# A fused attention and MLP kernel: another order table for its 1258 steps

## The chip, the cores and the metric

The kernel runs on one core of a Trainium2 chip. The metric is the time of one execution on the device in microseconds (us), the median of three runs. TensorE is called PE, VectorE DVE, ScalarE ACT, GpSimd POOL and SyncE SP, as in the profile.

## What is computed

The input `x` has 2048 tokens of 512 values. The result is `x + s * g`, where `s` is an attention over eight earlier tokens, two apart, and `g` a gated MLP, both of the same normalized input:

```python
xn = _layernorm(x)
qkv = (xn @ wqkv)                      # 32 heads of 16
logits = einsum("bhsd,bhswd->bhsw", q, kg) * scale   # kg: keys s, s-2, ..., s-14
o = einsum("bhsw,bhswd->bhsd", softmax(logits), vg)
s = o @ wo
y = _layernorm(xn)
g = silu(gelu(y @ w1 + b1) @ w2 + b2)  # 512 -> 1376 -> 512
return x + s * g
```

## The kernel before

Tokens are split by parity into two halves (c = 0, 1) of eight blocks of 128 tokens. Every multiplication of float32 values is made of three float16 ones: each operand is split into a high and a low part, scaled by a power of two that the kernel derives from a sum of squares (`total`, `half_exp`, `up`, `down`, L504 to L533).

The work comes in these pieces. `center` and `direct` (L673 to L691) make the first projections of two blocks directly in float32 from x, to give PE work while the other weights load. `y0` and `ln1` normalize the blocks and transpose them. `qkv` (L848 on PE) makes queries, keys and values of a unit, which is one half of the tokens and a group of eight heads; there are eight units. Its results leave PSUM by ACT (L866) or DVE (L862) into `U`. `attention` runs on DVE: products (L914), their sums (L917), softmax (L937 to L946, with the exponential on ACT, L940), products with the values (L972), sums of these shared by DVE (L967) and POOL (L982, L992), and a split for the output projection (L955 on ACT, L957 on DVE), whose result a DMA transposes (L960). `mlp1` (L1125 on PE, L1138 and L1141 on ACT, L1143 on DVE) and `mlp2` (L1161) are the MLP, for four chunks of 512 tokens and eleven slices of the hidden layer. `last_block` (L806 to L819; L806 and L807 pad on POOL) handles the narrow eleventh slice. `wo_first` and `wo_last` (L1038 and L1070 on PE) are the output projection.

`wo_last` ends the kernel. For each of the last eight blocks PE adds the last head group's share (L1070), DVE multiplies by the gate (L1102), DVE (L1109) or, for blocks 0, 2 and 4, POOL (L1106) adds x, and SP issues the store of the block (L1111). Block 7 is done in two halves of 256 columns, with a store each; the second one, the last half block, is multiplied in twelve matmuls of its own after everything else. So there are nine stores.

All DMAs are issued by SP. A DMA that waits for its data holds those behind it on SP. PSUM is used through rings of buffers: `ps` (three, for `qkv`, `mlp1` and some small totals), `pl` (one) and `z` (four). The products of attention use a ring of three buffers in SBUF (`prod`). 24 multiplications without use (L1279) fill PE's early waits.

The order of all this is not that of the code. `tile_mixer` only adds steps to a `Plan`, numbered in order of adding, each with its engine and what it reads and writes. `Plan.issue` then takes the steps in the order of the table `ORDER` and emits them; each engine executes its own steps in that order, and waits where data or a buffer isn't ready. When a step needs a new buffer of a ring, it gets the one that came free first by the table, so the table also decides which buffer serves what:

```python
order, fixed = [], [self.ops[n] for n in reversed(ORDER)]
...
            if fixed:
                o = fixed.pop()
```

Of the kernel before, what the change touches and what calls it, by code (L numbers as in the profile page):

```python
# [72 lines left out]
    0, 1, 2, 3, 4, 5, 6, 7, 8, 9, 10, 11, 19, 109, 117, 125, 114, 121, 130, 128, 108, 20, 123, 126, 129, 21, 33,  # L73
    32, 112, 22, 119, 23, 34, 24, 35, 25, 26, 54, 37, 38, 12, 13, 14, 15, 16, 17, 106, 107, 40, 49, 36, 68, 27,
    166, 47, 45, 41, 43, 28, 50, 51, 168, 115, 29, 30, 136, 31, 42, 53, 66, 56, 67, 69, 55, 57, 89, 167, 58, 62,
    70, 52, 71, 46, 72, 44, 90, 63, 169, 59, 137, 76, 64, 48, 18, 80, 170, 85, 65, 132, 73, 152, 74, 84, 86, 75,
    91, 87, 88, 60, 144, 178, 177, 138, 171, 139, 77, 173, 61, 153, 124, 154, 148, 149, 150, 120, 93, 78, 92,
    97, 98, 151, 175, 94, 81, 133, 99, 134, 174, 172, 181, 198, 95, 155, 82, 79, 145, 146, 116, 227, 228, 211,
    212, 213, 229, 214, 176, 182, 140, 141, 142, 179, 230, 135, 147, 100, 302, 96, 83, 306, 219, 203, 220, 221,
    143, 303, 304, 237, 180, 194, 196, 183, 156, 157, 158, 204, 205, 207, 208, 195, 197, 186, 190, 184, 159,  # L80
    305, 222, 187, 185, 39, 206, 191, 105, 160, 161, 192, 307, 308, 104, 101, 309, 102, 310, 314, 103, 238, 188,
    209, 210, 193, 385, 386, 199, 407, 200, 201, 408, 202, 242, 409, 111, 410, 113, 215, 216, 127, 400, 122,
    401, 217, 402, 110, 411, 412, 241, 218, 189, 239, 240, 387, 380, 413, 378, 403, 118, 414, 404, 415, 131,
    223, 243, 224, 225, 416, 417, 244, 405, 406, 256, 226, 246, 248, 382, 247, 249, 425, 441, 421, 422, 429,
# [12 lines left out]
    340, 344, 576, 526, 583, 567, 525, 341, 527, 647, 587, 646, 584, 597, 613, 342, 575, 348, 573, 615, 488,
    489, 598, 643, 586, 645, 644, 593, 654, 640, 1057, 641, 345, 594, 648, 349, 350, 614, 642, 346, 611, 612,
    652, 589, 595, 653, 660, 490, 596, 649, 590, 601, 602, 491, 351, 616, 618, 650, 617, 620, 619, 622, 347,
    499, 497, 353, 496, 352, 358, 514, 655, 651, 659, 591, 354, 355, 592, 656, 657, 623, 663, 661, 662, 671,  # L100
    668, 667, 670, 621, 626, 627, 628, 658, 492, 356, 624, 629, 630, 676, 599, 669, 678, 631, 632, 359, 664,
    672, 360, 665, 600, 679, 675, 677, 680, 673, 634, 633, 635, 361, 625, 357, 493, 606, 363, 362, 605, 579,
    368, 607, 681, 666, 637, 674, 682, 636, 683, 603, 685, 741, 737, 684, 686, 742, 694, 638, 604, 738, 364,
    695, 739, 692, 693, 365, 709, 710, 711, 366, 367, 609, 373, 577, 610, 608, 740, 712, 713, 688, 744, 757,
    748, 689, 758, 369, 746, 754, 743, 747, 749, 745, 702, 755, 753, 762, 773, 759, 714, 716, 715, 760, 718,
    719, 724, 717, 374, 375, 750, 370, 751, 725, 726, 371, 720, 721, 703, 727, 260, 722, 376, 372, 377, 723,
    728, 752, 729, 730, 690, 763, 756, 823, 764, 696, 691, 824, 698, 769, 697, 825, 699, 767, 771, 732, 731,
    733, 735, 826, 734, 736, 761, 829, 765, 700, 830, 837, 827, 828, 835, 831, 836, 701, 784, 832, 833, 704,
# [12 lines left out]
    1086, 1088, 1087, 1089, 1094, 1095, 1096, 961, 1019, 1097, 1090, 1032, 1030, 983, 924, 1020, 919, 925, 1098,
# [1351 lines left out]
```

## Time and profile before

| what | value |
|---|---|
| median of three runs (lowest to highest) | 420.45 us (419.94 to 420.98) |
| the profiled execution | 420.24 us |
| its span in the profile | 418.5 us |
| PE busy | 404.2 us, 97% |
| DVE busy | 386.4 us, 92% |
| ACT busy | 223.7 us, 53% |
| POOL busy | 129.3 us, 31% |
| DMA queue q1 | 51408 packets, 47.16 MB, 40.7% of 16 engines' span |

The span is the time from the first to the last recorded instruction of the core; the profiled execution's own time is 1.8 us longer. In a row of the timeline stand the start in us, the duration in us, the engine, the line of the kernel, the operation, what it writes and reads, and the count where like instructions were merged; in brackets at the end, how long the engine was idle before it and which instruction ended that. A row of the waits has who waited, for whom, the total in us, how many times, and the longest. A row of stretches has, after its length, the busy time of PE, PE's weight loads, DVE, ACT and POOL, then the granted clock of PE, the DMA share and GB/s. Starts of PE's multiplications overlap the ends of those before them by 0.16 us or so, since the array is a pipeline.

### The profile page before, as it was taken

What the parts mean: (1) busy time and instruction counts of PE and PEld (TensorE: products, weight loads), DVE (VectorE), ACT (ScalarE), POOL (GpSimd) and SP (SyncE); (2) the same over time, 40 slices, a digit from 0 to 9 for tenths busy, and PEclk for the clock granted to TensorE, in tenths of its full rate; (3) what the DMA queues carried; (4) which work ended last, traced back from release to release, by engine and by line L of the source; (5) the groups of instructions that cost most, each with busy time, mean ns of one, the idle gap of its engine ahead of it and who ended that gap; (6) DMA issues with size and microseconds to landing.
All of it is one profiled execution on the core that took longest, in us unless ns stands there. A gap on an engine that the chain in (4) does not pass through costs nothing.

```text
span 418.5 us, 5475 instructions
## 1 busy us (share of the span) xinstructions
PE 404.2 (97%) x2035; PEld 200.9 (48%) x2035; DVE 386.4 (92%) x379; ACT 223.7 (53%) x370; POOL 129.3 (31%) x140
## 2 busy tenths in 40 slices
PE   7999999999999999999999999999999999999991
PEld 4655544444444554554555554444455454444441
DVE  3998999999999999999989999999999989989972
ACT  3799998863768567435573361215432853162310
POOL 3820300061555352403333224232535250520021
PEclk9999999999999999999999999999999999999996
DMA  8938527340021372923148054310082439106334
GB/s 288 387 86 231 208 83 188 84 179 2 2 27 44 101 162 42 188 87 82 19 94 249 4 114 120 107 50 25 2 263 52 100 91 232 42 3 176 75 77 175
DMA packets 51435, 47.51 MB, mean 114 GB/s; under 512 B 36008, under 2 KB 36448, under 8 KB 50896
## 3 DMA queue, kind: packets, MB, share of 16 engines
q1 hardware_dynamic: 51408, 47.16, 40.7%
q8 instruction: 16, 0.26, 0.2%
q14 instruction: 11, 0.09, 0.1%
HBM read 24.11 MB, written 7.34 MB: 75 GB/s over the span
## 4 chain that ended last, share of the span: by engine, by line
PE 77%; DVE 15%; issue 4%; ACT 1%; DMA 1%; POOL 0%; DVEq 0%; ACTq 0%
PE ps L848 25%; PE z L1161 22%; PE ps L1125 18%; PE ps L1038 5%; PE ps L1070 2%; PE z L1070 2%; DVE L L917 2%; DVE w L560 2%; DVE prod L914 2%; DVE prod L972 2%; DVE h L1143 1%; PE pl L691 1%; DVE zsc L1349 1%; PE pl L848 1%; DVE wq L617 1%
## 5 line engine op out<-in xcount | busy, mean ns | idle before, releaser
L848 PE MATMUL ps<-wq,yT 128*128 128x384 f16 (+1 forms) x708 | 130.2, 337 | 0.9 <-DVE s L515 0.7
L1161 PE MATMUL z<-w,h 128*128 128x512 f16 x480 | 113.5, 379 | 0.0
L1125 PE MATMUL ps<-yT,w 128*128 128x512 f16 x480 | 110.4, 379 | 1.0 <-DVE ssq L515 1.0
L848 PEld LDWEIGHTS <-yT 128*128 128x128 f16 x744 | 72.5, 98 | 60.3 <-issue 1.8
L914 DVE TENSOR_TENSOR prod<-U 128x2048 f32<-128x2048 f32 x32 | 75.2, 2348 | 1.4
L1125 PEld LDWEIGHTS <-w 128*128 128x128 f16 x480 | 46.8, 98 | 56.2 <-issue 1.2
L917 DVE TENSOR_REDUCE L<-prod 128x128 f32<-128x2048 f32 x32 | 73.0, 2283 | 0.6
L1161 PEld LDWEIGHTS <-h 128*128 128x128 f16 x480 | 46.7, 98 | 54.3
L972 DVE TENSOR_TENSOR prod<-pl,U 128x2048 f32<-128x2048 f32 x28 | 63.4, 2283 | 3.1 <-POOL prod L982 2.8
L982 POOL TENSOR_TENSOR prod<-prod,prod 128x2048 f32<-128x2048 f32 x7 | 34.2, 4881 | 72.5 <-DVE prod L972 61.5
L1138 ACT ACTIVATE ps<-ps,b1T,hsc 128x512 f32<-128x512 f32 x40 | 29.7, 747 | 49.1 <-PE ps L1125 48.9
L866 ACT ACTIVATE U<-ps,cs 128x384 f32<-128x384 f32 x54 | 30.9, 576 | 38.4 <-PE ps L848 38.4
L991 POOL COPY gate<-prod 1x1 f32<-1x1 f32 x21 | 5.0, 240 | 112.2 <-DVE prod L914 102.0
L1141 ACT ACTIVATE h<-ps,hsc 128x512 f16<-128x512 f32 x40 | 27.1, 685 | 13.4 <-PE z L1161 12.1
L992 POOL TENSOR_TENSOR prod<-prod 128x1024 f32<-128x1024 f32 x14 | 32.9, 2348 | 0.0
L1143 DVE SCALAR_TENSOR_TENSOR h<-ps,hsc,h 128x512 f16<-128x512 f32 x40 | 29.4, 743 | 3.5 <-ACT h L1141 3.5
L1038 PE MATMUL ps<-wo,oT 128*128 128x512 f16 x96 | 21.9, 379 | 0.0
L967 DVE TENSOR_TENSOR prod<-prod,prod 128x2048 f32<-128x2048 f32 x9 | 20.6, 2290 | 0.2
L1138 ACT ACT_TABLE_LOAD x11 | 14.1, 1283 | 9.9 <-PE ps L1125 9.8
L955 ACT ACTIVATE o<-prod,osc 128x1024 f16<-128x1024 f32 (+1 forms) x9 | 9.4, 1049 | 15.6 <-DVE prod L967 10.3
L992 POOL TENSOR_TENSOR prod<-prod,prod 128x1024 f32<-128x1024 f32 x7 | 16.4, 2347 | 0.0
L1070 PEld LDWEIGHTS <-oT 128*128 128x128 f16 x108 | 10.6, 98 | 10.4
(188 smaller groups left out, 400.8 us busy)
## 6 DMA issues: line engine op xcount, KB each, us to landing
f<-in_A_x_dram SPq DMA_DIRECT2D x31, 256.0 KB, 3.2
U<-U SPq DMA_DIRECT2D x16, 392.0 KB, 3.9
gd<-f SPq DMA_DIRECT2D x12, 256.0 KB, 3.3
prod<-in_A_x_dram SPq DMA_DIRECT2D x8, 256.0 KB, 6.2
oT<-in_B_w_dram SPq DMA_DIRECT2D x2, 1024.0 KB, 9.8
yT<-in_B_w_dram SPq DMA_DIRECT2D x2, 1024.0 KB, 5.5
f<-gd SPq DMA_DIRECT2D x8, 256.0 KB, 3.4
out_dram<-f SPq DMA_DIRECT2D x8, 256.0 KB, 3.1
```

Source lines behind the costliest of these rows:

```text
L848: nc.tensor.matmul(b.t[:, 0:wide], y[:, s, k, o:o + P], wq[hb][:, t, k], start=(n == 0), stop=(n == 11))
L866: act(384, lambda i=i, b=b: nc.scalar.activation(U3[:, i:i + 31:15, :], b.t[:, 0:384].rearrange("p (t e) -> p t e", t=3), AF.Identity, sca ...
L914: dve(2048, lambda p2=p2, g=g: nc.vector.tensor_tensor(p2(), q, slots(Ut, KH, 2 * g), op=ALU.mult), qk + [("kh", ub, 0), ("kh", ub, 1), (" ...
L917: dve(2048, lambda pr=pr, g=g: nc.vector.tensor_reduce(L3()[:, 2 * g:2 * g + 2], pr.t.rearrange("p (r f d) -> p r f d", r=2, d=DH), AX.X, ...
L972: dve(2048, lambda: nc.vector.tensor_tensor(pr.t.rearrange("p (r f d) -> p r f d", r=2, d=DH), A3()[:, 2 * g:2 * g + 2].rearrange("p r (f ...
L982: pool(4.75, lambda: nc.gpsimd.tensor_tensor(acc.t, acc.t, p1.t, op=ALU.add), [acc, p1], [acc])
L992: nc.gpsimd.tensor_tensor(x.t[:, 0:1024], x.t[:, 0:1024], y(), op=ALU.add)
L1038: nc.tensor.matmul(b.t, oT[:, hb, i // 4, s, i % 4], wo[:, t, hb], start=(hb == 0 and n == 0), stop=(hb == last and n == 2))
L1125: nc.tensor.matmul(b.t[0:M], w1[:, s, f * 512 + k * M:f * 512 + (k + 1) * M], yT[ch][:, t, k], start=(n == 0), stop=(n == 11))
L1138: act(512, lambda: nc.scalar.activation(b.t[0:M], b.t[0:M], AF.Gelu_apprx_tanh, bias=b1T[0:M, f:f + 1], scale=hsc[0:M, 1:2]), [b, ("b1T",) ...
L1143: dve(512, lambda: nc.vector.scalar_tensor_tensor(lo()[0:M], b.t[0:M], hsc[0:M, 2:3], hi()[0:M], op0=ALU.mult, op1=ALU.subtract), [b, hk], ...
L1161: nc.tensor.matmul(z.t, hl[s][0:K, t * P:(t + 1) * P], w2[0:K, w, f], start=(f == 0 and n == 0), stop=(f == NF - 1 and n == 2))
```

## The change

The table `ORDER` is replaced by another order of the same 1258 numbers. Nothing else changes: the steps, their engines and what they compute are the same. The first and last lines of the table:

```diff
 ORDER = (
-    0, 1, 2, 3, 4, 5, 6, 7, 8, 9, 10, 11, 19, 109, 117, 125, 114, 121, 130, 128, 108, 20, 123, 126, 129, 21, 33,
+    0, 1, 2, 3, 4, 5, 6, 7, 8, 9, 10, 11, 19, 32, 33, 126, 128, 123, 115, 109, 20, 112, 114, 129, 21, 34, 22,
...
-    1237, 1256, 1252, 1228, 1257, 1248, 1223, 1253, 1243, 1233, 1238, 1218,
+    1233, 1218, 1248, 1243, 1223, 1253, 1254, 1255, 1256, 1237, 1238, 1257,
 )
```

What this moves on the engines is shown at three places.

SP, the nine stores that end the program (256 columns wide is a half of block 7, 512 a whole block). In brackets is what an instruction waits for, by engine; DMAHW is the queue's own place. Before:

```order
L1111 DMA out_dram<-U_88 128x512 [waits DMAHW2_49,Pool_49]
L1111 DMA out_dram<-U_88 128x256 [waits DMAHW3_49,DVE_49,Activation_49]
L1111 DMA out_dram<-U_88 128x512 [waits DMAHW4_49]
L1111 DMA out_dram<-U_88 128x512 [waits DMAHW5_49]
L1111 DMA out_dram<-U_88 128x256 [waits DMAHW6_49,DVE_49]
L1111 DMA out_dram<-U_88 128x512 [waits DMAHW7_49]
L1111 DMA out_dram<-U_88 128x512 [waits DMAHW0_49]
L1111 DMA out_dram<-U_88 128x512 [waits DMAHW1_49,Pool_49]
L1111 DMA out_dram<-U_88 128x512 [waits DMAHW2_49]
```

And now:

```order
L1111 DMA out_dram<-U_88 128x512 [waits DMAHW2_49,Pool_49]
L1111 DMA out_dram<-U_88 128x512 [waits DMAHW3_49,DVE_49]
L1111 DMA out_dram<-U_88 128x512 [waits DMAHW4_49,Pool_49]
L1111 DMA out_dram<-U_88 128x512 [waits DMAHW5_49,DVE_49]
L1111 DMA out_dram<-U_88 128x512 [waits DMAHW6_49,DVE_49]
L1111 DMA out_dram<-U_88 128x512 [waits DMAHW7_49]
L1111 DMA out_dram<-U_88 128x256 [waits DMAHW0_49,DVE_49]
L1111 DMA out_dram<-U_88 128x512 [waits DMAHW1_49,Pool_49]
L1111 DMA out_dram<-U_88 128x256 [waits DMAHW2_49,DVE_49]
```

The store of the last half block (step 1257) was second and is now last; that of block 4 (1238, added by POOL) was eighth and stands before it. By block the order was 2, last half, 6, 1, first half of 7, 5, 3, 4, 0, and is 2, 3, 0, 6, 5, 1, first half of 7, 4, last half. On PE, the three half-wide multiplications of the first half of block 7 (step 1250) stood between the last ones of block 4 (1235) and the final twelve (1254), and now stand before block 4's.

DVE, where the first attention unit meets the first `mlp1` steps (about 42 to 54 us before). L914 and L917 are products and sums of the attention, L1143 is the end of an `mlp1` step and frees its PSUM buffer. Before:

```order
L914 TENSOR_TENSOR prod_95<-U_88 128x2048
L917 TENSOR_REDUCE L_105<-prod_95 128x2x64
L931 MEMSET L_105 1x8
L914 TENSOR_TENSOR prod_96<-U_88 128x2048
L1143 SCALAR_TENSOR_TENSOR h_109<-ps_143,hsc,h_109 128x512
L914 TENSOR_TENSOR prod_97<-U_88 128x2048
```

And now:

```order
L914 TENSOR_TENSOR prod_96<-U_88 128x2048
L917 TENSOR_REDUCE L_105<-prod_96 128x2x64
L914 TENSOR_TENSOR prod_95<-U_88 128x2048
L917 TENSOR_REDUCE L_105<-prod_95 128x2x64
L1143 SCALAR_TENSOR_TENSOR h_109<-ps_142,hsc,h_109 128x512
L931 MEMSET L_105 1x8
```

A second L917 now stands ahead of the first L1143, which moved behind it. On PE the buffer ps_142 that this L1143 reads is taken next by an L848 group of two sets of four (steps 215 and 216), and four sets of three L1125 (400 to 403) and three sets of four L848 (223 to 225), which stood behind this group, now stand ahead of it.

DVE somewhat later (about 72 to 92 us before). L515 on `ssq` reads a total from a `ps` buffer and so frees it for PE. Before:

```order
L942 TENSOR_REDUCE mx_112<-L_105 128x64
L617 SCALAR_TENSOR_TENSOR wq_79<-yT_86,qsc,wq_79 128x2x384
L943 RECIPROCAL mx_112<-mx_112 128x64
L946 TENSOR_TENSOR pl_144<-L_105,mx_112 128x512
L972 TENSOR_TENSOR prod_97<-pl_144,U_88 128x2048
L617 SCALAR_TENSOR_TENSOR wq_79<-yT_86,qsc,wq_79 128x2x384
L1143 SCALAR_TENSOR_TENSOR h_110<-ps_141,hsc,h_110 128x512
L972 TENSOR_TENSOR prod_96<-pl_144,U_88 128x2048
L1143 SCALAR_TENSOR_TENSOR h_109<-ps_142,hsc,h_109 128x512
L1349 TENSOR_TENSOR zsc<-zsc,hsc 128x1
L917 TENSOR_REDUCE L_106<-prod_95 128x2x64
L515 TENSOR_SCALAR ssq<-ps_143 128x1
```

And now:

```order
L946 TENSOR_TENSOR pl_144<-L_105,mx_112 128x512
L1143 SCALAR_TENSOR_TENSOR h_108<-ps_142,hsc,h_108 128x512
L917 TENSOR_REDUCE L_106<-prod_95 128x2x64
L515 TENSOR_SCALAR ssq<-ps_142 128x1
L522 TENSOR_SCALAR s_124<-ssq 128x1
L528 TENSOR_SCALAR qsc<-s_124 128x1
L533 TENSOR_SCALAR qsc<-s_124 128x1
L1143 SCALAR_TENSOR_TENSOR h_110<-ps_143,hsc,h_110 128x512
L972 TENSOR_TENSOR prod_97<-pl_144,U_88 128x2048
L972 TENSOR_TENSOR prod_96<-pl_144,U_88 128x2048
L1143 SCALAR_TENSOR_TENSOR h_109<-ps_141,hsc,h_109 128x512
L1349 TENSOR_TENSOR zsc<-zsc,hsc 128x1
```

The `ssq` reduction moved ahead of two L972, two L1143 and L1349. The next total that PE waited for (L515 on `s`, the output weights') moved ahead of other such work as well.

Elsewhere the table differs on every engine. Of that the prediction speaks of two more places: at the start, the reductions of the first weights' total (L504, L515 on `ssq`) stand on PE and DVE ahead of the float32 multiplications L691 that they stood between, and five of the 24 multiplications L1279 stand ahead of the first L682 instead of eight; and on POOL the second pair L806, L807 stands ahead of the second L982, behind which it stood.

118 rows, old and new, of the table ORDER are left out of this document.

## The prediction

> **What bounds the kernel now.** I read the page first, then busy time by stretches, then the waits, and last the timeline of the two ends.
>
> ```profile
> PE 404.2 (97%) x2035; PEld 200.9 (48%) x2035; DVE 386.4 (92%) x379; ACT 223.7 (53%) x370; POOL 129.3 (31%) x140
> ```
>
> ```profile
> 55.00:60.00 5.00, 5.00 (x25) 2.24 (x24) 5.00 (x4) 4.94 (x11) 0.00 (x0) 1.00 0.00 0
> ...
> 110.00:200.00 90.00, 90.00 (x455) 44.32 (x454) 87.20 (x69) 55.58 (x92) 36.45 (x39) 1.00 0.39 85
> 200.00:300.00 100.00, 99.98 (x506) 49.39 (x505) 95.86 (x73) 41.69 (x62) 30.72 (x36) 1.00 0.31 82
> 300.00:400.00 100.00, 100.00 (x490) 47.71 (x488) 95.04 (x72) 41.84 (x58) 29.43 (x31) 1.00 0.41 108
> ...
> 410.00:418.50 8.50, 0.00 (x0) 0.00 (x0) 1.19 (x3) 0.00 (x0) 0.40 (x1) 0.62 0.59 216
> ```
>
> In a stretch's row the first pair is PE, the third DVE. From 110 to 400 us PE is busy for 289.98 of 290, and a new order takes no multiplication away, so nothing can be won there, only lost. What an order can win lies at two ends: PE waits before 110, and the 8.5 us at the end in which PE does nothing. The waits of PE:
>
> ```profile
> PE ps L682 <- DVE f L676: 1.6, 1, 1.6
> ...
> PE z L691 <- DVE U L684: 0.8, 1, 0.8
> ...
> PE ps L1125 <- DVE ssq L515: 1.0, 1, 1.0
> ...
> PE ps L848 <- DVE s L515: 0.7, 1, 0.7
> ```
>
> The first follows the first load and stays. The last two (at 90.0 and 99.0 us), 1.7 us together, come late because DVE is full there (5.00 of 5 in the first stretch quoted): from 35 to 130 us DVE, not PE, is behind.
>
> **The end.** DVE's and PE's last rows, SP's first and last store, SP's longest wait and the landing time:
>
> ```profile
> 406.58 1.29 DVE L1109 TENSOR_TENSOR U<-U,f 128x512 f32<-128x512 f32 x2
> 408.31 1.14 DVE L1102 SCALAR_TENSOR_TENSOR U<-z,osc,U 128x512 f32<-128x512 f32 x2 [0.43 <-PE z L1070]
> 408.43 1.47 PE L1070 MATMUL ps<-wo,oT 128*128 128x256 f16 x12
> 409.14 1.26 POOL L1106 TENSOR_TENSOR U<-U,f 128x512 f32<-128x512 f32 x1 [7.20 <-DVE U L1102]
> 409.94 0.48 DVE L1102 SCALAR_TENSOR_TENSOR U<-ps,osc,U 128x256 f32<-128x256 f32 x1 [0.49 <-PE ps L1070]
> 410.46 0.76 DVE L1109 TENSOR_TENSOR U<-U 128x256 f32<-128x256 f32 x2
> ```
>
> ```profile
> 410.95 0.34 SPq L1111 DMA_DIRECT2D out_dram<-U  x1
> ```
>
> ```profile
> 411.35 3.58 SPq L1111 DMA_DIRECT2D out_dram<-U  x7
> ```
>
> ```profile
> SPq L1111 <- DVE U L1109: 9.9, 1, 9.9
> ```
>
> ```profile
> DMA to landing us min/median/max: 2.8/3.0/3.0
> ```
>
> PE's last multiplication ends at 409.90; the span ends 8.6 us later. SP issues in program order, and its second store is that of the last half block. It waits 9.9 us for the very last data (the first of the two adds from 410.46), and seven stores stand behind it; the adds of five of them were done by 407.9 (406.58 + 1.29). So eight stores leave one after another, 410.95 to 414.93 (0.34 + 3.58 us), the last starts at 414.3, lands 3.0 us later at 417.3, and 1.2 us of closing follow.
>
> **The change at the end.** By SP's rows the store of the last half block is now last and the other half of block 7 third from the end; between them stands block 4, which POOL adds. Let E be the end of the last multiplication. Block 4's last three multiplications now stand directly before PE's final twelve (the three half-wide ones of block 7 moved ahead of them), and those twelve take 1.47 us. So DVE's L1102 of block 4 runs from E-1.4 to E-0.6 (the pair takes 1.14, the full-width one of it some 0.75), and POOL's L1106 of 1.26 ends at E+0.75. SP issues that store at E+0.8, with 0.48 to the next (eight stores in 3.9 us now), and the last half block, whose add is done at E+1.0 now (SP's 410.95), at E+1.3. It lands by E+4.3, and with 1.2 of closing the span ends at E+5.5 instead of E+8.6: **-3.1 us**. The others are ready from E-7 to E-0.1 and leave one at a time before. Bounds: if the half-size store lands 0.5 sooner, -3.6; if block 4's path or stores crowding at the end add 0.6, -2.5. The Trainium skill, DMA: Bandwidth & Descriptors, section Anatomy of one DMA, gives a fixed 2.0 us plus bytes over 436 GB/s, an estimate of 2.3 us for 128 KB and a gain of 3.8; this trace measures 2.8 to 3.0 for stores of this line, so I keep the rows.
>
> **The change before 110 us.** The `ssq` reduction (L515 on ps) that PE's L1125 waits for stands behind two products (L972, 2.3 us each), two L1143 and L1349 now, and ahead of them in the new order: 2 x 2.3 + 2 x 0.74 + 3.96 = 10 us of DVE work. The second L515 moves up as well, by some 6. Both waits, **-1.7 us**, are gone unless something else is late. Something is: the first L1143 gets one more L917 ahead of it.
>
> ```profile
> 84.73 3.96 DVE zsc L1349
> ```
>
> ```profile
> L917 DVE TENSOR_REDUCE L<-prod 128x128 f32<-128x2048 f32 x32 | 73.0, 2283 | 0.6
> ```
>
> ```profile
> 46.94 3.33 DVE L914 TENSOR_TENSOR prod<-U 128x2048 f32<-128x2048 f32 x1
> 46.95 0.07 DVE L931 MEMSET L<- 1x8 f32 x1
> 50.20 0.74 DVE L1143 SCALAR_TENSOR_TENSOR h<-ps,hsc,h 128x512 f16<-128x512 f32 x1
> ```
>
> ```profile
> 45.09 1.46 PE L848 MATMUL ps<-wq,yT 128*128 128x384 f16 x8
> ...
> 46.50 0.81 PE L1125 MATMUL ps<-yT,w 128*128 128x512 f16 x3
> ...
> 49.31 0.81 PE L1125 MATMUL ps<-yT,w 128*128 128x512 f16 x3
> ...
> 51.47 0.81 PE L848 MATMUL ps<-wq,yT 128*128 128x384 f16 x4
> ...
> 52.22 1.46 PE L848 MATMUL ps<-wq,yT 128*128 128x384 f16 x8
> 53.52 6.64 PE L1125 MATMUL ps<-yT,w 128*128 128x512 f16 x30
> ```
>
> L917 takes 2.2 us here (2.28 in the group's mean, overlapping the next by 0.1), so L1143 starts at 50.2 + 2.2 = 52.4 if DVE is otherwise as far, and ends at 53.1. It frees the PSUM buffer of the L848 group that stands at 45.09 now. Ahead of this group PE now has four sets of three L1125 (46.50 to 49.31, 0.65 each, as thirty take 6.5) and three sets of four L848 (51.47 and 52.22, 0.65 each), 4.6 us, with 0.4 of fill-in multiplications: PE is there at about 50.1 and waits up to 3. From its start to E lie now 409.9 - 45.1 = 364.8 us, less 1.7 of waits and 5.0 of work that goes ahead of it: 358.1. So E = 53.1 + 358.1 = 411.2, **+1.3**, and the two old waits lie inside it. How far DVE is by then depends on waits in front of it:
>
> ```profile
> DVE ssq L515 <- PE z L504: 1.1, 1, 1.1
> ...
> DVE w L560 <- ACT w L556: 0.8, 1, 0.8
> ...
> DVE s L513 <- PE z L509: 0.4, 1, 0.4
> ```
>
> The first of these reductions now precedes the first direct multiplications (L691) on PE, so DVE gets it sooner. All three back, 2.3 us, would put L1143 where it was and leave only 1.7 to gain; none back gives +1.3. I take about half back: L1143 ends at 52.05, E = 410.15, **+0.3**.
>
> The fill-in multiplications (L1279, 24 as before): five instead of eight stand ahead of the first L682, where PE waits for the load anyway; three more now fall between later groups. I set that at nothing: they go where PE waits for DVE in any case, and without that cover three cost three half-size multiplications, less than the 0.4 us counted for four above.
>
> **The sum.** It is made against the profiled execution, 420.24 us (span 418.5 and 1.8 around it), which lies 0.2 under the median of 420.45 and inside the runs' spread: 420.24 - 3.1 + 0.3 = **417.4 us**. Bounds of the two terms together: 420.24 - 3.6 - 1.7 = 414.9, and 420.24 - 2.5 + 1.3 = 419.0.
>
> **Rivals.** (1) *DVE is early enough*: all of its front waits return, both PE waits go and the L1143 is no wait: 420.24 - 3.1 - 1.7 = 415.4. For it speaks that the reductions move up by 6 to 10 us; against it that DVE has no idle time between 35 and 130 us, so that only work it does earlier can shorten it.
>
> (2) *PE's slow start lasts longer.* PE is slow at first:
>
> ```profile
> 6.21 1.65 PE L691 MATMUL pl<-prod,U 128*128 128x384 f32 x2
> ...
> 7.87 1.49 PE L691 MATMUL pl<-prod,U 128*128 128x384 f32 x2
> ...
> 9.22 0.91 PE L691 MATMUL pl<-prod,U 128*128 128x384 f32 x2
> ```
>
> A pair of L691 takes 1.65 and 1.49 us, and 0.91 from 9.2 on. With three fewer multiplications ahead and a pause at the moved reduction, the fast rate may come later; two more pairs (0.6 each) and the eight L673 behind them (1.0) at the slow rate delay DVE's second L684 and all behind it by 2.2: 417.4 + 2.2 = 419.6. The Trainium skill, TensorE: Matmul & The Clock Gate, Part 1, has that rule: an array that idled runs at half clock until it has been busy for about one window of 3.4 us. The trace agrees with the halved rate; what counts as busy no run here shows.
>
> (3) *The other side: POOL holds DVE in the middle.* DVE has waited for POOL's L982, which frees a product buffer:
>
> ```profile
> 129.74 5.42 POOL L982 TENSOR_TENSOR prod<-prod,prod 128x2048 f32<-128x2048 f32 x1 [8.22 <-DVE prod L972]
> ...
> 145.51 2.95 POOL L807 TENSOR_SCALAR f<-halves,hsc 128x4 f16<-128x4 f32 x1
> ```
>
> ```profile
> 135.20 2.29 DVE L972 TENSOR_TENSOR prod<-pl,U 128x2048 f32<-128x2048 f32 x1 [0.92 <-POOL prod L982]
> ```
>
> In the new order the second pair L806, L807 (0.3 before the 2.95 us) stands ahead of that L982 instead of behind it. If its inputs come late, POOL starts the add 3.3 later, and DVE, with L1143 and the PSUM buffers behind it, 4.2 after it asked. PE has three such buffers, each a group of twelve (2.6 us of L1125), and DVE has 2.8 us idle in 110 to 200; beyond those the time goes to PE one for one. Such a wait at two places with 2 to 2.5 us left over at each gives 417.4 + 4.5 = 421.9. It makes the kernel slower from 2.8 + 1.3 us of new PE waits after 110 on (2.8 is what the forecast gains). Against it: POOL is idle for 8.2 us before that L982 now.
>
> (4) *The stores are no limit after all*: something else holds them at the end, as a load or POOL's add of block 2, which the first store waits for. Only 0.5 of the 3.1 is left: 420.0.
>
> **How the numbers follow.** Forecast 417.4: 0.48, with a range of its own of 415.9 to 419.0. (1) 415.4: 0.24. (2) 419.6: 0.07. (3) 421.9: 0.14. (4) 420.0: 0.07. A measurement of this kernel tells 0.3%, 1.3 us, from no change: faster is under 419.2. Faster: the forecast, (1), and a little of (2): 0.74; within: the rest of (2) and (4): 0.13; slower: (3) less a tail: 0.13. The range has to leave no more than 0.2 out: from 414.8 (both terms at their best) to 420.4 it keeps all cases but (3) and the tails.
>
> **What would show it.** Right: the first seven of SP's L1111 stores issued before PE's last multiplication ends, the last store within 1.5 us after, and 5 to 6 us between PE's end and the span's end; no PE wait at L515 near 90 or 99; a wait of PE at an L848 near 50 us on DVE's h L1143 of up to 3 us. Wrong: a PE end beyond 411.5, above all by idle PE time between 110 and 400, or eight stores in a row after PE's end again.

## The result and the profile after

| | before | changed |
|---|---|---|
| median, 20 runs each (us) | 420.26 (419.53 to 421.04) | 420.87 (420.09 to 421.62) |
| ratio to before, 95% interval | | 1.0014 [1.0006, 1.0022] |
| span of the profiled execution (us) | 418.5 | 419.1 |
| end of PE's last multiplication (E) | 409.90 | 414.59 |
| from E to the end of the span | 8.6 | 4.5 |

Forecast were 417.4 us and E = 410.2. The end of the kernel gained more than the forecast's 3.1 us, namely 4.1, but PE came to that end 4.7 us later than before, and so the kernel is 0.6 us slower. First the end: the timeline of the changed kernel from PE's last twelve multiplications on (start, duration, engine, line).

```profile
413.12 1.47 PE L1070 MATMUL ps<-wo,oT 128*128 128x256 f16 x12
...
413.98 0.42 DVE L1109 TENSOR_TENSOR U<-U 128x256 f32<-128x256 f32 x1
414.15 1.38 POOL L1106 TENSOR_TENSOR U<-U,f 128x512 f32<-128x512 f32 x1 [3.85 <-DVE U L1102]
414.63 0.48 DVE L1102 SCALAR_TENSOR_TENSOR U<-ps,osc,U 128x256 f32<-128x256 f32 x1 [0.22 <-PE ps L1070]
415.14 0.66 DVE L1109 TENSOR_TENSOR U<-U 128x256 f32<-128x256 f32 x1
```

SP's own queue, the nine stores as one row, and then the seventh and the last of them from narrower stretches:

```profile
407.99 8.37 SPq L1111 DMA_DIRECT2D out_dram<-U  x9
```

```profile
414.43 0.33 SPq L1111 DMA_DIRECT2D out_dram<-U  x1
```

```profile
415.97 0.38 SPq L1111 DMA_DIRECT2D out_dram<-U  x1
```

The seventh store is issued at 414.43, before E = 414.59, and the last at E + 1.4. From issue to landing the stores now take 2.0 us, against 2.8 to 3.0 before:

```profile
DMA to landing us min/median/max: 2.0/2.0/2.5
```

Where did the 4.7 us in front of E go? Busy time by stretches, PE the first pair, the granted clock the figure behind POOL's pair:

```profile
45.00:60.00 15.00, 14.66 (x76) 7.15 (x75) 11.34 (x14) 14.34 (x21) 4.16 (x1) 1.00 0.07 27
60.00:80.00 20.00, 20.00 (x97) 9.11 (x96) 19.90 (x23) 16.54 (x30) 0.59 (x6) 1.00 0.65 175
80.00:100.00 20.00, 17.14 (x76) 7.37 (x75) 19.83 (x21) 14.71 (x32) 6.34 (x3) 0.91 0.31 108
...
170.00:200.00 30.00, 28.21 (x140) 13.43 (x138) 29.61 (x16) 12.81 (x23) 7.00 (x3) 1.00 0.39 87
200.00:400.00 200.00, 200.00 (x1000) 97.60 (x998) 190.16 (x141) 85.83 (x123) 60.81 (x68) 1.00 0.38 99
```

PE is idle for 2.86 us in 80 to 100 and for 1.79 in 170 to 200, and in the first of these the clock is not 1.00. DVE is idle for 3.66 us in 45 to 60. The first place, DVE and POOL and PE together:

```profile
87.28 0.74 DVE L1143 SCALAR_TENSOR_TENSOR h<-ps,hsc,h 128x512 f16<-128x512 f32 x1
87.45 4.51 POOL L982 TENSOR_TENSOR prod<-prod,prod 128x2048 f32<-128x2048 f32 x1 [20.14 <-DVE prod L972]
...
87.94 4.04 DVE L1349 TENSOR_TENSOR zsc<-zsc,hsc 128x1 f32<-128x1 f32 x1
88.63 0.19 PE L504 MATMUL ps<-s,fours 128*128 128x1 bf16 x2
88.69 2.75 PE L1161 MATMUL z<-w,h 128*128 128x512 f16 x12
...
91.90 2.27 DVE L972 TENSOR_TENSOR prod<-pl,U 128x2048 f32<-128x2048 f32 x1
...
94.10 0.14 DVE L515 TENSOR_SCALAR s<-ps 128x1 f32<-128x1 f32 x1
```

PE's L504 (the total of the output weights) takes a PSUM buffer and is done at 88.82. DVE's L515, which reads it and so frees the buffer, stands in DVE's order behind L1349 and an L972 and comes at 94.10: the buffer is held for 5.3 us. L1349 has 4.04 of them, though it has one column only: it ends together with POOL's L982 (91.98 and 91.96), and takes 0.16 us where POOL is idle (below). In the kernel before, the same pair lay 1.8 us apart (L504 until 97.67, L515 at 99.48), from which came PE's old wait of 0.7:

```profile
97.50 0.17 PE L504 MATMUL ps<-s,fours 128*128 128x1 bf16 x1
...
99.48 0.15 DVE L515 TENSOR_SCALAR s<-ps 128x1 f32<-128x1 f32 x1
```

In the changed kernel PE needs the buffer at 91.44:

```profile
94.30 4.44 PE L1125 MATMUL ps<-yT,w 128*128 128x512 f16 x12 [2.86 <-DVE s L1388]
```

Twelve such multiplications take 2.75 us at full clock (in the kernel before, for one). (The row names L1388, the instruction behind L515; in the run with L515 moved, below, L1125 starts at 90.58 and L1388 runs at 93.42, so it is L515 that frees the buffer.) The granted clock by single microseconds says why they take longer:

```profile
94.00:95.00 1.00, 0.70 (x4) 0.31 (x4) 1.00 (x5) 0.29 (x2) 0.00 (x0) 0.95 0.11 33
95.00:96.00 1.00, 1.00 (x4) 0.41 (x3) 1.00 (x4) 0.00 (x0) 0.00 (x0) 0.50 0.92 244
96.00:97.00 1.00, 1.00 (x4) 0.29 (x2) 1.00 (x1) 0.00 (x0) 0.00 (x0) 0.50 0.01 2
97.00:98.00 1.00, 1.00 (x4) 0.34 (x3) 1.00 (x3) 0.00 (x0) 0.00 (x0) 0.50 0.00 0
98.00:99.00 1.00, 1.00 (x5) 0.40 (x4) 1.00 (x4) 0.23 (x1) 0.00 (x0) 0.84 0.00 0
```

It fell to a half for 3.4 us (twice the missing shares 0.05, 0.5, 0.5, 0.5 and 0.16), which costs 1.7. By the first of these shares it fell at 94.9, 0.6 us after PE had begun again. Wait and clock together: 4.55 us. The second place:

```profile
174.16 4.50 POOL L982 TENSOR_TENSOR prod<-prod,prod 128x2048 f32<-128x2048 f32 x1 [11.06 <-DVE prod L972]
174.18 5.03 DVE L787 TENSOR_TENSOR f<-f,f 128x512 f16<-128x512 f32 x1 [0.17 <-ACT f L786]
...
179.13 0.74 DVE L1143 SCALAR_TENSOR_TENSOR h<-ps,hsc,h 128x512 f16<-128x512 f32 x1
...
179.93 2.11 PE L848 MATMUL ps<-wq,yT 128*128 128x384 f16 x12 [1.48 <-DVE h L1143]
```

An L787 that takes 0.67 us at 183.3 takes 5.03 here. It starts 0.02 us behind POOL's L982 and ends 0.55 behind it, and the L1143 for which PE waits stands behind it. With 0.32 for the next L1161 (at 182.8) this is 1.8 us. In the kernel before, this L787 also stood right behind two L972, but it started 0.23 us ahead of L982 and was not held:

```profile
172.07 0.68 DVE L787 TENSOR_TENSOR f<-f,f 128x512 f16<-128x512 f32 x1
172.30 4.84 POOL L982 TENSOR_TENSOR prod<-prod,prod 128x2048 f32<-128x2048 f32 x1 [10.98 <-DVE prod L972]
```

In the changed kernel it waited 0.17 us for ACT's L786, and so came second.

The account of E: 4.55 and 1.8 lost, 0.34 more at an L848 at 50.2, less the two old waits of 1.7: +5.0, of which 4.69 shows. The remaining 0.3 was not traced row by row; behind 45 us no other wait of PE and no other slow stretch shows, so by elimination it lies in the start. What the trace alone does not decide is *which* of these rows is cause and which only lies on the way. DVE's longest new wait, for one, was 3.52 us at L513 (53.67), and it looked to me like the beginning of it all.

### The profile page after: what moved, and what is told of

Same layout as the page of the kernel before. It is cut to its first block, busy times and chain, and to the rows that moved or that the text cites. A ratio compares the mean times of both kernels' runs of the same rounds, so it can differ in the third digit from the quotient of the medians.

```text
span 419.1 us, 5490 instructions
## 1 busy us (share of the span) xinstructions
PE 405.6 (97%) x2035; PEld 200.9 (48%) x2035; DVE 387.8 (93%) x379; ACT 225.6 (54%) x371; POOL 128.9 (31%) x140
## 4 chain that ended last, share of the span: by engine, by line
PE 89%; DVE 9%; DMA 1%; issue 0%; ACT 0%; SPq 0%; DVEq 0%
PE ps L848 27%; PE z L1161 26%; PE ps L1125 23%; PE ps L1038 5%; PE ps L1070 2%; PE z L1070 2%; DVE prod L972 2%; DVE L L917 1%; PE pl L691 1%; DVE w L560 1%; DVE prod L914 1%; DVE zsc L1349 1%; DMA prod<-in_A_wqkv_dram 1%; DVE h L1143 1%; PE pl L848 1%; PE z L691 1%
## 5 line engine op out<-in xcount | busy, mean ns | idle before, releaser
L848 PE MATMUL ps<-wq,yT 128*128 128x384 f16 (+1 forms) x708 | 130.6, 337 | 1.8 <-DVE h L1143 1.5
L1125 PE MATMUL ps<-yT,w 128*128 128x512 f16 x480 | 111.5, 383 | 2.9 <-DVE s L1388 2.9
L1161 PE MATMUL z<-w,h 128*128 128x512 f16 x480 | 113.0, 379 | 0.3 <-DVE h L1143 0.3
L848 PEld LDWEIGHTS <-yT 128*128 128x128 f16 x744 | 72.3, 98 | 61.4 <-issue 2.4
L1125 PEld LDWEIGHTS <-w 128*128 128x128 f16 x480 | 47.3, 99 | 59.5 <-issue 5.3
L914 DVE TENSOR_TENSOR prod<-U 128x2048 f32<-128x2048 f32 x32 | 73.9, 2308 | 1.9 <-DMA U<-U 1.0
L917 DVE TENSOR_REDUCE L<-prod 128x128 f32<-128x2048 f32 x32 | 73.1, 2285 | 0.8
L1161 PEld LDWEIGHTS <-h 128*128 128x128 f16 x480 | 46.5, 98 | 54.6 <-DVE h L1143 0.8
L972 DVE TENSOR_TENSOR prod<-pl,U 128x2048 f32<-128x2048 f32 x28 | 63.2, 2282 | 3.2 <-POOL prod L982 2.9
L982 POOL TENSOR_TENSOR prod<-prod,prod 128x2048 f32<-128x2048 f32 x7 | 34.4, 4921 | 82.9 <-DVE prod L972 82.9
L1143 DVE SCALAR_TENSOR_TENSOR h<-ps,hsc,h 128x512 f16<-128x512 f32 x40 | 29.5, 744 | 1.8 <-ACT h L1141 1.6
L1106 POOL TENSOR_TENSOR U<-U,f 128x512 f32<-128x512 f32 x3 | 4.3, 1428 | 34.5 <-DVE U L1102 34.5
```

What stands on the lines that cost most here:

```text
L848: nc.tensor.matmul(b.t[:, 0:wide], y[:, s, k, o:o + P], wq[hb][:, t, k], start=(n == 0), stop=(n == 11))
L914: dve(2048, lambda p2=p2, g=g: nc.vector.tensor_tensor(p2(), q, slots(Ut, KH, 2 * g), op=ALU.mult), qk + [("kh", ub, 0), ("kh", ub, 1), (" ...
L917: dve(2048, lambda pr=pr, g=g: nc.vector.tensor_reduce(L3()[:, 2 * g:2 * g + 2], pr.t.rearrange("p (r f d) -> p r f d", r=2, d=DH), AX.X, ...
L972: dve(2048, lambda: nc.vector.tensor_tensor(pr.t.rearrange("p (r f d) -> p r f d", r=2, d=DH), A3()[:, 2 * g:2 * g + 2].rearrange("p r (f ...
L982: pool(4.75, lambda: nc.gpsimd.tensor_tensor(acc.t, acc.t, p1.t, op=ALU.add), [acc, p1], [acc])
L1125: nc.tensor.matmul(b.t[0:M], w1[:, s, f * 512 + k * M:f * 512 + (k + 1) * M], yT[ch][:, t, k], start=(n == 0), stop=(n == 11))
```

## The experiments

Ratios are to runs of the kernel before on the same chip, with 95% intervals; three chips were used, so rows are compared by their ratios. A median is of four executions, or of nine or ten (L509 and L914 earlier; L787 later; free columns). Single executions differ by up to 2.4 us in when PE comes through the first loads (the first L1125 behind 36 us starts at 37.3 in one profile, at 39.7 in another, in kernels whose order is the same up to there). So for the kernels with the new order I also give the distance from PE's L504 (the 88.63 above) to E, from the profiles: 325.96 us in the changed kernel.

| kernel | median (us) | ratio, interval | L504 to E (us) |
|---|---|---|---|
| old order, stores moved, with a slip | 418.27 | 0.9955 [0.9938, 0.9973] | |
| old order, stores moved | 417.15 | 0.9932 [0.9913, 0.9952] | |
| new order, L509 and L914 earlier | 420.65 | 1.0016 [1.0005, 1.0027] | 325.96 |
| new order, L1349 elsewhere | 416.90 | 0.9921 [0.9905, 0.9937] | 321.24 |
| new order, four L1161 sets ahead of L1125 | 416.60 | 0.9919 [0.9905, 0.9934] | 321.40 |
| new order, L515 earlier | 415.76 | 0.9896 [0.9880, 0.9913] | 321.30 |
| new order, L787 later | 418.93 | 0.9965 [0.9952, 0.9977] | 322.15 |
| new order, 24 fill-ins, used buffer | 428.48 | 1.0196 [1.0178, 1.0214] | |
| new order, 24 fill-ins, free columns | 419.37 | 0.9977 [0.9966, 0.9989] | 324.28 |
| new order, L515 and L787 | 416.50 | 0.9903 [0.9886, 0.9920] | 321.29 |
| new order, L515, L787 and L1349 | 414.80 | 0.9867 [0.9847, 0.9888] | 319.11 |
| old order, stores and L1349 | 415.16 | 0.9875 [0.9860, 0.9890] | |

**Was the gain at the end real?** The first try to give the old order only the new order of stores:

> The old order, with only SP's eight output stores behind the first in the new order (the half block's last). Theory T (the end alone gained what the prediction said): PE's last multiplication stays at 409.9, the stores of blocks 3, 0, 6, 5, 1 leave before it, the last store at about 412.1 instead of 414.3, and the span ends 4.5 to 5.5 us behind PE's end instead of 8.6: 416.3 to 417.2 us, ratio 0.990 to 0.993. Rival (the stores are no limit, the gain at the end of the changed kernel is only its later PE): 419.5 to 420.5, ratio 0.998 to 1.000.

It gave 1.9 us. But my edit had put the store of block 2 (step 1228) last as well, instead of first, so that four stores still left behind the data of the half block, the last at 413.6. The run fits neither theory's range. The edit as meant:

```diff
-    1215, 1225, 1199, 1198, 1159, 1220, 1207, 1201, 1200, 1209, 1230, 1208, 1160, 1161, 1239, 1226, 1227, 1245,
-    1221, 1216, 1231, 1232, 1222, 1217, 1240, 1206, 1235, 1250, 1246, 1241, 1242, 1247, 1254, 1236, 1251, 1255,
-    1237, 1256, 1252, 1228, 1257, 1248, 1223, 1253, 1243, 1233, 1238, 1218,
+    1215, 1225, 1199, 1198, 1159, 1220, 1207, 1201, 1200, 1209, 1230, 1208, 1160, 1161, 1239, 1226, 1227, 1228, 1245,
+    1221, 1216, 1231, 1232, 1233, 1222, 1217, 1218, 1240, 1206, 1235, 1250, 1246, 1241, 1242, 1247, 1248, 1243, 1223, 1254, 1236, 1251, 1255,
+    1237, 1256, 1252, 1253, 1238, 1257,
```

> The old order, with only SP's nine output stores put in the new order, block 2 first and the half block last (in the run before, block 2's store had slipped to the end by my edit, so that the last store left at 413.6). Theory T: PE's end stays where it was, the last store is issued about 2.2 us behind it, and the span ends 5.6 us behind PE's end instead of 8.6: 3.0 us less, 416.9 to 417.5 us, ratio 0.992 to 0.9935. Rival (the stores' order is worth only what the slipped run gained, 1.9 us, since something else holds the end): ratio 0.995 to 0.996.

Its timeline at the end, PE and then SP, and the landing time of its stores:

```profile
408.19 1.47 PE L1070 MATMUL ps<-wo,oT 128*128 128x256 f16 x12
```

```profile
411.04 1.30 SPq L1111 DMA_DIRECT2D out_dram<-U  x3
```

```profile
DMA to landing us min/median/max: 2.1/2.1/3.2
```

E = 409.66, three stores instead of eight behind it, and the span of 415.1 ends at E + 5.4 (forecast: 5.5, but by other terms; see the point on the end below). The stores' order alone is worth 0.68%, about 2.9 us. The other 0.9 us that the changed kernel has at its end (4.5 against 5.4) comes with the order on PE and DVE there: block 7's first half is added before the half block's last multiplication is evicted (the row at 413.98 is that add), not behind it. That part is read from the rows and was not tried by itself.

**Does DVE's 3.5 us wait at L513 make it late at 94?** Two numbers moved: PE's L509 (243) three sets earlier, one L914 (378) in front of the fused L513 (244).

```diff
-    400, 380, 381, 385, 386, 413, 387, 226, 238, 239, 242, 113, 401, 402, 403, 215, 216, 414, 415, 217, 404,
-    405, 218, 243, 244, 406, 378, 416, 417, 441, 425, 248, 311, 246, 418, 249, 247, 254, 419, 252, 164, 262,
+    400, 380, 381, 385, 386, 413, 387, 226, 238, 239, 242, 113, 401, 402, 403, 215, 216, 414, 243, 415, 217, 404,
+    405, 218, 378, 244, 406, 416, 417, 441, 425, 248, 311, 246, 418, 249, 247, 254, 419, 252, 164, 262,
```

> The new order, with the reduction L509 on PE three sets earlier (in front of a set of three L1125) and one product L914 on DVE in front of the fused L513 instead of behind L1143. Theory A (DVE's idle 3.5 us at L513 is what makes it late at 94): the idle time falls to under 0.5 us, DVE is 3 us earlier at 94, PE's wait of 2.9 falls to 0 to 0.3 and the clock stays at 1.00: 416.2 to 416.8 us, ratio 0.990 to 0.992. Rival B (PE asks for the buffer too early even with DVE on time, since other work was moved ahead of the step that frees it): the wait stays above 1.5 us, 419.5 to 421.

The wait at L513 went, and nothing else did. DVE's rows of this run further on:

```profile
56.09 1.28 DVE L560 SCALAR_TENSOR_TENSOR w<-yT,zsc,w 128x1024 f16<-128x1024 f32 x1 [1.27 <-ACT w L556]
57.73 1.28 DVE L560 SCALAR_TENSOR_TENSOR w<-yT,zsc,w 128x1024 f16<-128x1024 f32 x1 [0.36 <-ACT w L556]
```

```profile
70.77 0.16 DVE L515 TENSOR_SCALAR ssq<-ps 128x1 f32<-128x1 f32 x1 [1.32 <-PE ps L504]
```

DVE now waits for ACT and, at 70.77, for a total that PE delivers when PE's own order has it. By there the time won is gone, L504 to E is 325.96 us in both kernels, and PE waits 2.87 us as before. Theory A, as I had put it, falls, and 420.65 us lies in the range of rival B: the largest new wait in DVE's list cost nothing.

**What does make it late, and is it lateness at all?** Three edits, each at another link. First, DVE's work in front of 94: the one-column L1349 (245), 4.04 us long, goes behind the fused L513 (244).

```diff
-    405, 218, 243, 244, 406, 378, 416, 417, 441, 425, 248, 311, 246, 418, 249, 247, 254, 419, 252, 164, 262,
+    405, 218, 243, 244, 245, 406, 378, 416, 417, 441, 425, 248, 311, 246, 418, 249, 247, 254, 419, 252, 164, 262,
...
-    320, 452, 286, 287, 540, 541, 542, 543, 396, 245, 322, 398, 288, 537, 289, 557, 538, 291, 539, 256, 558,
+    320, 452, 286, 287, 540, 541, 542, 543, 396, 322, 398, 288, 537, 289, 557, 538, 291, 539, 256, 558,
```

> The new order, with the one-column multiplication of zsc by hsc (L1349), which took 4.04 us on DVE from 87.9 on, beside POOL's L982, moved right behind the fused reduction that makes zsc (54.4). Theory A (DVE is late at 94, whatever made it late, and PE's wait of 2.9 us and its half clock for 3.4 us follow from that): the multiplication takes 0.1 us, DVE frees the buffer at about 90.3, the wait is 0 and the 12 L1125 take 2.75 us again: PE's end 4.5 earlier, 416.3 us, ratio 0.990 to 0.992. Rival B (the L1125 waits for something else than DVE's lateness): 420 to 421. Rival D (L972 behind it is held by POOL in its place): 419 to 420.

There it takes 0.16 us:

```profile
55.29 0.16 DVE L1349 TENSOR_TENSOR zsc<-zsc,hsc 128x1 f32<-128x1 f32 x1
```

Second, PE's side: the group of twelve L1125 (544) behind four sets of L1161 (548 to 551) that are ready.

```diff
-    293, 559, 257, 397, 290, 259, 399, 502, 503, 544, 549, 551, 548, 550, 479, 323, 321, 324, 326, 325, 545,
+    293, 559, 257, 397, 290, 259, 399, 502, 503, 549, 551, 548, 550, 544, 479, 323, 321, 324, 326, 325, 545,
```

> The new order, with the four sets of three L1161 that follow the waiting group of twelve L1125 (94.3) put in front of it; their operand has been ready since 83. Theory A: PE fills 2.6 of the 2.9 us, the wait falls to about 0.3 and the clock stays at 1.00; DVE stays late, so the L848 behind (waits for DVE's L972 at 98.0) takes back about 1 us: PE's end 3.3 to 4.3 earlier, 416.6 to 417.6 us. Rival B' (the time is lost by DVE's total work in front of 98, wherever PE waits): the wait moves whole to the L848, 419 to 420.

PE's rows of this run, with the wait down to 0.27 and the twelve back at 2.75 us:

```profile
88.70 5.34 PE L1161 MATMUL z<-w,h 128*128 128x512 f16 x24
94.31 2.75 PE L1125 MATMUL ps<-yT,w 128*128 128x512 f16 x12 [0.27 <-DVE s L515]
```

Third, only the one instruction that frees the buffer, L515 (288), goes in front of L1349 and L972. DVE's work in front of 94 stays what it was.

```diff
-    320, 452, 286, 287, 540, 541, 542, 543, 396, 245, 322, 398, 288, 537, 289, 557, 538, 291, 539, 256, 558,
+    320, 452, 286, 287, 288, 540, 541, 542, 543, 396, 245, 322, 398, 537, 289, 557, 538, 291, 539, 256, 558,
```

> The new order, with one DVE instruction moved: the L515 that reads PSUM (total of the sums of wo) stands right behind the L1143 at 87.3, in front of L1349 (4.0 us) and one L972 (2.2 us), where its input from PE is ready (88.83). Theory H (the buffer is held: PE's L504 takes it at 88.7, and DVE's own order frees it only 5.3 us later; DVE's idle time at 50 us is no part of it): the wait of 2.9 us and the half clock go, 416.2 to 416.9 us, ratio 0.990 to 0.992. Rival A' (DVE's total lateness decides, so the wait goes to the next buffer, the L848 behind L972): 418.5 to 420, ratio 0.996 to 1.000.

```profile
87.94 0.19 PE L504 MATMUL ps<-s,fours 128*128 128x1 bf16 x2
88.00 2.75 PE L1161 MATMUL z<-w,h 128*128 128x512 f16 x12
88.21 0.16 DVE L515 TENSOR_SCALAR s<-ps 128x1 f32<-128x1 f32 x1 [0.88 <-PE ps L504]
88.29 3.00 DVE L1349 TENSOR_TENSOR zsc<-zsc,hsc 128x1 f32<-128x1 f32 x1
90.58 2.75 PE L1125 MATMUL ps<-yT,w 128*128 128x512 f16 x12
```

DVE even waits 0.88 us for PE at L515, the buffer is free at 88.4, and PE's L1125 follows without a gap. All three edits shorten L504 to E by 4.6 to 4.7 us. To within 0.2 us, the first does it by these 4.55 alone, the other two by them and the second loss, which they happen to avoid (below), less new waits of PE near 105, 1.6 us with the L1161 moved and 1.9 with L515. So it is the place of L515 (theory H): one small instruction behind 6.2 us of work, 3.9 of them only L1349 being held by POOL. Either alone, L515 in front or L1349 elsewhere, ends the wait.

**The second loss: the L787 of 174.2.** Step 361 goes behind the next L1143s (674, 666, 682).

```diff
-    679, 678, 663, 669, 667, 675, 677, 676, 630, 631, 664, 665, 680, 681, 632, 634, 633, 361, 635, 674, 637,
-    666, 682, 366, 636, 638, 605, 362, 606, 625, 367, 608, 603, 684, 742, 737, 686, 685, 683, 741, 744, 604,
+    679, 678, 663, 669, 667, 675, 677, 676, 630, 631, 664, 665, 680, 681, 632, 634, 633, 635, 674, 637,
+    666, 682, 361, 366, 636, 638, 605, 362, 606, 625, 367, 608, 603, 684, 742, 737, 686, 685, 683, 741, 744, 604,
```

> The new order, with one L787 (f32 minus f16, 0.67 us elsewhere) moved from right behind two L972, where it ran beside POOL's L982 and took 5.03 us (174.2), to behind the next three L1143. Theory P (it was held for as long as POOL's instruction ran, and PE's wait of 1.48 us at the L848 of 179.9 and of 0.32 at the L1161 of 182.8 follow): it takes 0.7 us, both waits go: 1.8 us less, 418.9 to 419.3 us, ratio 0.996 to 0.998. Rival Q (PE's wait at 179.9 comes from DVE's work as a whole, as three L972 beside L982): the wait stays, 420.5 to 421, ratio 1.000 to 1.002.

```profile
174.18 4.54 POOL L982 TENSOR_TENSOR prod<-prod,prod 128x2048 f32<-128x2048 f32 x1 [10.60 <-DVE prod L972]
174.62 2.28 DVE L972 TENSOR_TENSOR prod<-pl,U 128x2048 f32<-128x2048 f32 x1
175.07 3.40 PE L1161 MATMUL z<-w,h 128*128 128x512 f16 x15
178.31 2.11 PE L848 MATMUL ps<-wq,yT 128*128 128x384 f16 x12
179.74 1.28 DVE L787 TENSOR_TENSOR f<-f,f 128x512 f16<-128x512 f32 x2
```

Two L787 in 1.28 us, no gap on PE, 1.9 us less than the changed kernel's 420.87: theory P holds. (L504 to E is 3.8 shorter in this profile: 1.8 by these waits and some 1.7 since its clock did not fall at the first place, see the last section; 0.3 are not traced.) Note the L972, whose one input lies in PSUM (pl): beside the same L982 it takes its usual 2.28.

**Wait and clock apart.** 24 extra fill-in multiplications in front of the waiting L1125, their results never read.

> The new order unchanged, with 24 more multiplications of the fill-in kind on PE (into the unused pl buffer, results never read) between the L1161 that ends at 91.4 and the group of twelve L1125 that waits until 94.3. Theory C (the idle time itself lets the clock fall to a half, and that costs 1.7 us behind the wait): the L1125 still start at 94.3, the granted clock stays at 1.00 from 94 to 100, the twelve take 2.75 us instead of 4.44: 1.7 us less, 419.0 to 419.4 us, ratio 0.996 to 0.998. Rival (the half clock has another cause, or the wait is longer for it): 420.5 to 421, ratio 1.000 to 1.002.

```profile
99.00 4.95 PE L1124 MATMUL pl<-first,fours 128*128 128x256 bf16 x24 [6.62 <-DVE prod L972]
```

This says nothing about the clock. The buffer I had taken for free holds the probabilities that DVE's L972 reads until 98, and PE waited 6.62 us for it. The same again into columns of the total's own bank that nobody uses:

```diff
-            pe(3, 512, mm, [h, hk, w2key[f]], [zt[t]])
+
+            def more(mm=mm):
+                mm()
+                for n in range(24):
+                    nc.tensor.matmul(R_ps.tiles[0][:, 2 * P:4 * P], fours, mean1.bitcast(BF16), start=True, stop=True)
+            pe(3, 512, more if (ch, f, t) == (0, 6, 3) else mm, [h, hk, w2key[f]], [zt[t]])
```

> The same question as the run with 24 fill-in multiplications before, whose buffer turned out to be in use: now they write columns 256 to 511 of the bank of which L504 and L515 use column 0, behind the last L1161 at 91.4 (results never read). Theory C (PE's idle time of 2.9 us is what lets the clock fall to a half): they run from 91.4 to 94.1, the L1125 start at 94.3 as before, the granted clock stays at 1.00 and the twelve take 2.75 instead of 4.44 us: 1.7 less than the changed kernel's 420.9, 419.0 to 419.4 us, ratio 0.996 to 0.998. Rival (the half clock has another cause): 420.5 to 421, ratio 1.000 to 1.002.

```profile
91.45 2.78 PE L1167 MATMUL ps<-first,fours 128*128 128x256 bf16 x24
94.49 2.75 PE L1125 MATMUL ps<-yT,w 128*128 128x512 f16 x12 [0.25 <-DVE s L1393]
```

The L1125 start no earlier, but take 2.75 us; L504 to E shortens by 1.68. So theory C holds: without the idle time the clock does not fall here, and that is worth 1.5 (by the medians) to 1.7 us.

**Both mended, and the best.** L515 and L787 moved together:

> The new order with both places mended: L515 (the sums of wo) in front of L1349 and L972, and the L787 of 174.2 behind the three L1143. If the two losses (4.6 and 1.8 us at PE's end) are separate, as theories H and P have them: 415.8 less 1.8, 413.8 to 414.4 us, ratio 0.984 to 0.987. If the second was already taken up by DVE's earlier state in the run with the first mended: 415.4 to 415.9, ratio 0.988 to 0.990.

With 321.29 us from L504 to E it is the same as with L515 alone (321.30), and the ratios agree within their intervals: the second loss was not there any more. (416.50 us itself lies above both ranges; the profiled run came late out of the first loads, with L504 at 90.35.) In the run with L515 alone, the L787 had come 0.23 us *before* POOL's L982 instead of 0.02 behind it:

```profile
171.13 0.68 DVE L787 TENSOR_TENSOR f<-f,f 128x512 f16<-128x512 f32 x1
171.36 4.84 POOL L982 TENSOR_TENSOR prod<-prod,prod 128x2048 f32<-128x2048 f32 x1 [10.32 <-DVE prod L972]
```

With L1349 moved as well, the two waits of 1.0 and 0.9 us that remained (at an L848 and an L1161 near 105) go:

> As the run with both places mended, and L1349 moved right behind the fused L513, where POOL is idle: DVE has 3 us less to do in front of 95, and the waits of 0.96 us at an L848 (105.5) and 0.9 at an L1161 (for a DMA of hl) that the run with L515 moved showed. If they are DVE's lateness: 412.5 to 413.5 us, ratio 0.981 to 0.984. If PE is the limit already: as the run with both places mended, 413.8 to 414.4.

414.80 us, 1.3% under the kernel before. L504 to E is 2.2 us shorter than with two, and PE is without a gap from 60 us to E, so the waits were DVE's lateness. The time does not decide it: it is 1.3 above the range that I gave for that case and 0.4 above the other's, and the profiled run came late out of the first loads (L504 at 89.92). The same two ideas in the old order, its stores and its L1349 moved:

> The old order with the nine stores in the new order (417.15 us by themselves) and L1349 (4.04 us beside POOL's L982 at 84.65) moved right behind the fused L513. Theory P (held only beside POOL): it takes 0.15 us, DVE is 3.9 us earlier at 90, PE's two waits of 0.8 and 0.7 us go: 415.4 to 415.8 us, ratio 0.988 to 0.990. Rival (the waits come from something else in front of L515): 416.9 to 417.3, ratio 0.992 to 0.9935.

L1349 takes 0.16 us there too, PE's waits at 90 and 99 are gone, and 415.16 us can't be told from 414.80. Both kernels beat the kernel before and the changed one.

## Why the prediction was wrong, point by point

- **The bound** (PE has nothing to win between 110 and 400, only to lose; two ends can be won) was right. 1.8 us were lost there.
- **The end, -3.1 us**: mechanism right, size too small, by one term. The last store left at E + 1.4, where the sum had it (E + 1.3). Too long was what follows: 3.0 us of landing and 1.2 of closing, from the rows of before (414.28 to 418.5), where now 3.1 in all pass (415.97 to 419.1), since a store lands in 2.0. So the end is worth -4.1. With the stores' order alone, E + 5.4 instead of the forecast's 5.5 was luck: there the last store left at 411.90, E + 2.2, 0.9 later than in the sum, and landed 1 us sooner. Why stores landed later in the kernel before stays open; a crowd of stores behind E is not enough, since four in a row land in 2.0 to 2.2 us in the run with the slip. The estimate of 2.3 us that the prediction set aside was nearer, though the Trainium skill (DMA: Bandwidth & Descriptors, Anatomy of one DMA) gives that formula for DMAs issued through GpSimd, and these are SP's.
- **The front, +0.3 us: here the prediction failed**, in the step "the two old waits lie inside it", that is, that both PE waits at L515 go because the reductions stand earlier on DVE. The wait at 90 did go. The L515 on `s` does stand earlier, by 5.4 us (99.48 to 94.10), but PE's L504, which takes the buffer, moved ahead by 8.8 (97.50 for the second of the pair to 88.66), so the hold grew from 1.8 to 5.3 us, and PE's wait there from 0.7 to 2.86, 4.55 with the clock behind it. The order of DVE was compared with DVE's order of before, and not with what PE had now put in front. The upper end of the range (+1.3) rested on the L848 near 50 alone and had no term for that, and the sum none for the middle, where 1.8 us were lost.
- **The clock** was in no term behind the start: the price of a wait was taken as its length. This one cost 1.6 times that (4.55 for 2.86).
- **The L848 near 50 us**, up to 3 us expected, cost 0.34: the L1143 behind the second L917 ended at 50.14, not at 52 to 53, since DVE waited less in the front (busy for 19.32 us of 20 to 40, before 18.08).
- **Rival 3** (POOL's L806, L807 hold the second L982 and DVE behind it) did not happen: POOL was idle for 8.20 us in front of that L982, and DVE's waits for L982 add up to 2.9 us now and 2.8 before. Its place and its direction were right, by another mechanism: L982 held DVE's L787 with no dependence between them, because that came 0.02 us behind it, in the kernel before 0.23 ahead.
- **Rival 2** (a longer slow start): the second and third pair of L691 together take 2.50 us, before 2.26 (7.87 to 10.13), so 0.2 us more and not 2.2. (The granted clock is listed as 1.00 in the first 20 us of both profiles and does not show the slow pairs.) The slow stretch that cost time came at 95. **Rivals 1 and 4** fall with the rows above.
- Put together: 417.4 forecast, 1.0 more gained at the end, 4.55 lost at 94, which makes 420.95, the profiled execution's own time. That the front's +0.3 and the middle's 1.8 need no further term is partly luck: the L848 near 50 was cheaper by 1.6, and there are the 0.3 of the account.

## What to carry to other kernels

When an order changes, compare for each buffer the time between the instruction that takes it and the one that frees it, on the two engines together; a small instruction that frees something belongs in front of long ones for which nobody waits. The longest new wait in the list need not be the cause (3.5 us at L513 cost nothing), and a cause need not be in the list at all: time for which DVE's instruction is held by POOL's counts as its own busy time (L787, 5.03 us), so look for durations that do not fit a size. And price PE's idle time of a few microseconds with the half clock that can follow it (1.7 us here).

## What the runs showed of the hardware

- **DVE held by POOL.** DVE's L787 and L1349, with both inputs in SBUF, are done only when POOL's L982 has ended, if they start while it runs: L787 5.03 us instead of 0.68, L1349 (one column) 4.04 and 3.00 instead of 0.16. Instructions with an input in PSUM (L972, L1143) are not held, 2.28 and 0.74 beside the same L982. The other way round, POOL's L982 took 4.84 instead of 4.50 where the L787 had started first. The Trainium skill, SBUF — State Buffer, section SBUF: two separate sides, has this rule: the two engines share a pair of ports, and whichever of a POOL instruction and a DVE instruction with two SBUF inputs starts first has it for its whole length. The trace agrees in both directions. It was in the kernel before, too, at L1349 (4.04 us from 84.65), which cost it some 2 us (with the stores moved, ratio 0.9932 to 0.9875).
- **The clock falls behind less than 3 us of idle time, but not always.** After 2.86 and 2.87 us (the changed kernel, and the one with L509 and L914 earlier) the twelve L1125 took 4.44 and 4.16 us; after 2.88 us, in the profiled run with L787 moved, they took 2.75 (its row stands at the end). The waits of 0.96 and 0.71 before left the clock at 1.00. How often it fell can be read from the mean clock of an execution, of which this place takes 0.004 (1.7 of 419 us) and the end behind E up to 0.003 in the profiles here (4.6 us at 0.74, in the kernel with L515, L787 and L1349 moved): 17 of the changed kernel's 20 have 0.995 or 0.996, three have 0.999. Those three took 420.09, 420.32 and 420.38 us, only 0.7 less than the median of the others, so the price of 1.5 to 1.7 rests on the fill-ins. The Trainium skill, TensorE: Matmul & The Clock Gate, Part 1, has the clock fall after an idle window of about 3.4 us, and the windows run freely. That equal waits end differently, and that the half clock lasted 3.4 us, agrees; that an idle time shorter than the window was enough does not follow from it, and here the measurement decides. The row with 2.88 us of idle time and a full clock, from the kernel with L787 moved:

```profile
96.01 2.75 PE L1125 MATMUL ps<-yT,w 128*128 128x512 f16 x12 [2.88 <-DVE s L515]
```
